# A decode kernel: wo's first 20 heads in one load, part of V's last tile as 112, 8 and 8 partitions, q made as rows, two heads' sums folded together

## The chip, the cores and the metric

The kernel runs on one core of a Trainium2 chip. The metric is the device time of one execution in microseconds (us), as the median of several runs; less is better. The core has five engines with queues of their own: TensorE (PE in the profile, with PEld for its weight loads), VectorE (DVE), ScalarE (ACT), GpSimd (POOL) and SyncE (SP). SP issues nearly all DMAs of this kernel; the DMA engines, 16 of them, carry them out.

## The reference

One token attends to a cache, beside a small feed-forward block, and a gate mixes the two. All data are bf16.

```python
# x: [1, 1, 512]; k_cache, v_cache: [1, 32, 65536, 128]; wq: [512, 4096]; wo: [4096, 512]
# w_gate, w_up: [512, 1792]; w_down: [1792, 512]; gate_w: [512]
q = (x @ wq).reshape(1, 1, 32, 128)                       # 32 heads
p = softmax(einsum(q, k_cache) * 128 ** -0.5)             # per head, over 65536 keys
a = einsum(p, v_cache).reshape(1, 1, 4096) @ wo
b = (silu(x @ w_gate) * (x @ w_up)) @ w_down
g = sigmoid((x * gate_w).sum(-1, keepdims=True))
out = g * a + (1 - g) * b
```

The two caches are 1,074 MB, and each element is used once. The whole input is 1,088 MB.

## The kernel before

**Tiling.** A head's keys are split over the 128 partitions, 512 to each, and a head is done in G = 2 tiles of SIZE = 256 keys per partition. So there are N = 64 tiles of K and 64 of V, each 128 partitions x 64 KB (8 MB). They go through a ring of SLOTS = 3 buffers of that size. A buffer is free again when the last instruction that reads its tile has ended, and `load` then issues the next tile's DMA from SP. The order of all work is written out by hand; each engine does its instructions in program order.

**The loop** (line 485) runs over n = 0 to 63. Iteration n loads K's tile n and V's tile n - 2 (LEAD = 2). `products` multiplies the K tile in place with q, which `query_spread` has copied to all partitions, on VectorE, and folds the 128 products of a key to 16 by three additions (lines 258 and 262). `scores` adds those 16 up and moves them to PSUM with eight matmuls (line 271); after them the K tile's buffer is free. `add_up` makes the scores of them. When a head's two tiles are scored (n even), `row_max` and `exponentials` make the softmax weights P_sb. They are placed behind the first multiplication of the next K tile; for that the tile is cut in rows 0 to 64 and 64 to 256. `values` multiplies a V tile with P_sb in 64 matmuls of four columns (line 340), which go to four strips of O_ps in turn; after them the V tile's buffer is free.

**A head's end.** `head_copy` copies O_ps to SBUF; `head_sum` adds its pieces up with four matmuls against `pick` (float32: each is two instructions), for one head at a time. `head_row` scales the head's row of 128 and puts it into a row of QUAD = 4 heads; `turn` turns four heads' row into columns of oT by small matmuls, as the lhsT that `into_row` needs for the projection with wo.

**wo** (4,096 rows of 512, 1 KB each) comes in four parts. Heads 0 to 3 (FIRST, 512 rows) are loaded in mid-run by `load_tall`: after the V loads at ten values of n, four DMAs each, of 5, 3 or 1 partitions four apart, in rows of 3 to 5 KB; `tall_row` and `tall_zero` clear their buffers on GpSimd, `turn_first` turns these heads' values, and `project_tall` projects them. Heads 4 to 19 (LONG) are one load of 128 rows of 16 KB, after the last V tile but one; 20 to 27 (PAIR) and 28 to 31 (LAST) come at the end.

**q.** `query_columns` makes q as 32 columns, one per head, with 128 matmuls of one column; `query_spread` makes a diagonal matrix from a head's column on ScalarE (diag_q) and copies it to all partitions with one matmul.

**The end** (from line 534). The last V tile is loaded in three parts by V_CUTS, 168, 64 and 24 keys per partition (rows of 43,008, 16,384 and 6,144 B), behind LONG's wo, then PAIR and LAST. `values` runs part by part, O_ps is folded on VectorE (line 574), the last head's value goes to oT, the rest of wo is projected, and the row is copied and stored.

Of the kernel before, what the change touches and what calls it, by code (L numbers as in the profile page):

```python
# [11 lines left out]
P = 128  # L12
# [12 lines left out]
FIRST, LONG, PAIR, LAST = (0, 4), (4, 20), (20, 28), (28, 32)  # L25

SHARES = ((5, 3), (3, 15), (1, 4))
TALL_ROUNDS = ((2, 0, 4), (1, 0, 5), (1, 5, 10), (1, 10, 15), (0, 0, 3))
TALL_LOADS = {14: 0, 23: 1, 32: 2, 41: 3, 50: 4}
TALL_PROJECTS = {18: 0, 27: 1, 36: 2, 45: 3, 54: 4}  # L30
# [3 lines left out]
def kernel(  # L34
# [31 lines left out]
    qT = edge.tile([P, H], f32, name="qT")  # L66
# [22 lines left out]
    x_row = consts.tile([1, D], bf16, name="x_row", tag="o_row")  # L89
# [4 lines left out]
    def load(dst, cache, n, name, cuts=None):  # L94
        t, taken[name, n] = big(name)
        view = t.rearrange("p (j d) -> p j d", d=Dh)
        src = cache[0, n // G, :, :].rearrange("(p j) d -> p j d", p=P)
        a = n % G * SIZE
        cuts = cuts or (0, SIZE)
        for c, d in zip(cuts[:-1], cuts[1:]):  # L100
            nc.sync.dma_start(out=view[:, c:d, :], in_=src[:, a + c : a + d, :])
        dst[n] = view
# [30 lines left out]
    def query_columns(first, last):  # L133
        q_ps = psum_m.tile([P, last - first], f32, name="q_ps", tag="misc")
        for h in range(first, last):
            for t in range(KT):
                nc.tensor.matmul(
                    q_ps[:, h - first : h - first + 1],
                    lhsT=wq_sb[:, t, h * Dh : (h + 1) * Dh],
                    rhs=xT[:, t : t + 1],  # L140
                    start=(t == 0),
                    stop=(t == KT - 1),
                )
        nc.scalar.activation(out=qT[:, first:last], in_=q_ps, func=ACT.Copy)
# [3 lines left out]
    def query_spread(h):  # L148
        diag_q = consts.tile([P, Dh], bf16, name="diag_q")
        nc.scalar.activation(out=diag_q, in_=ident_b, func=ACT.Copy, scale=qT[:, h : h + 1])  # L150
        qb_ps = psum_m.tile([P, Dh], f32, name="qb_ps", tag="misc")
        nc.tensor.matmul(qb_ps, lhsT=ones_b, rhs=diag_q, start=True, stop=True)  # L152
        q_tiles[h] = pair.tile([P, Dh], bf16, name="q_sb")
        nc.scalar.activation(out=q_tiles[h], in_=qb_ps, func=ACT.Copy)  # L154
# [3 lines left out]
    query_columns(0, 1)  # L158
    query_spread(0)
    query_columns(1, H)  # L160
# [18 lines left out]
    gw_row = consts.tile([1, D], bf16, name="gw_row", tag="tall")  # L179
# [69 lines left out]
    def products(n, a, b):  # L249

        K = K_tiles[n][:, a:b, :]
        qb = q_tiles[n // G]
        q_rep = bass.AP(
            tensor=qb.tensor,
            offset=qb.offset,
            ap=[list(qb.ap[0]), [0, b - a], [1, Dh]],
        )
        yield nc.vector.tensor_tensor(out=K, in0=K, in1=q_rep, op=ALU.mult)  # L258
# [92 lines left out]
    def head_copy():  # L351
        O_sb = consts.tile([P, QUAD * Dh], f32, name="O_sb")
        nc.scalar.activation(out=O_sb, in_=O_ps, func=ACT.Copy)  # L353
        return [O_sb[:, c * Dh : (c + 1) * Dh] for c in range(QUAD)]

    def head_sum(h, parts):
        if h >= LAST[0]:
            r_ps = psum_r.tile([P, 1], f32, name="r_ps")
            for c in range(QUAD):
                nc.tensor.matmul(  # L360
                    r_ps, lhsT=parts[c], rhs=pick[:, c : c + 1], start=(c == 0), stop=(c == 3)
                )
            return r_ps
        r_ps = psum_r.tile([1, Dh], f32, name="r_ps")
        for c in range(QUAD):
            nc.tensor.matmul(  # L366
                r_ps, lhsT=pick[:, c : c + 1], rhs=parts[c], start=(c == 0), stop=(c == 3)
            )
        return r_ps


    row0 = 0
    TP = 32 + 4 * SHARES[0][0]
    assert sum(2 * 4 * ports * deep for ports, deep in SHARES) == QUAD * P
    TR = max(b - a for _, a, b in TALL_ROUNDS)
    pieces, bases = [], []
    width = 0
    for ports, deep in SHARES:
        bases.append(width)
        for half in range(2):  # L380
            pieces.append((row0, row0 + 4 * ports * deep, width + 32 * half * deep))
            row0 += 4 * ports * deep
        width += TP * deep
    tallT = consts.tile([TP, sum(deep for _, deep in SHARES)], bf16, name="tallT")
    tall = {}

    def tall_row():
        tall["row"] = consts.tile([1, width], bf16, name="tall_row", tag="tall")
        nc.gpsimd.memset(tall["row"], 0.0)

    def tall_zero():
        tall["sb"] = consts.tile([TP, TR, D], bf16, name="tall_sb", tag="tall")
        nc.gpsimd.memset(tall["sb"], 0.0)

    def load_tall(r, half):
        s, a, b = TALL_ROUNDS[r]
        ports, deep = SHARES[s]
        first = pieces[2 * s + half][0]
        for i in range(4):
            src = bass.AP(  # L400
                tensor=A_wo.tensor,
                offset=A_wo.offset + (first + i * deep + a) * D,
                ap=[[4 * deep * D, ports], [1, (b - a) * D]],
            )
            lo = 32 * half + i
            nc.sync.dma_start(
                out=tall["sb"][lo : lo + 4 * (ports - 1) + 1 : 4, : b - a].rearrange(
                    "p t n -> p (t n)"
                ),
                in_=src,  # L410
            )

    def project_tall(r):
        s, a, b = TALL_ROUNDS[r]
        rows = 32 + 4 * SHARES[s][0]
        at = sum(deep for _, deep in SHARES[:s])
        for t in range(b - a):
            into_row(tallT[:rows, at + a + t : at + a + t + 1], tall["sb"][:rows, t, :])
# [3 lines left out]
    def head_row(h, r_ps):  # L422
# [4 lines left out]
        if h < FIRST[1]:  # L427
            for a, b, at in pieces:
                lo, hi = max(a, h * Dh), min(b, h * Dh + Dh)
                if lo < hi:  # L430
                    nc.scalar.activation(
                        out=tall["row"][:, at + lo - a : at + hi - a],
                        in_=r_ps[:, lo - h * Dh : hi - h * Dh],
                        func=ACT.Copy,
                        scale=gate[0:1, :],
                    )
            return
        if h % QUAD == 0:
            rows[h // QUAD] = consts.tile([1, QUAD * Dh], bf16, name="o_row")
        at = (h % QUAD) * Dh  # L440
        nc.scalar.activation(
            out=rows[h // QUAD][:, at : at + Dh], in_=r_ps, func=ACT.Copy, scale=gate[0:1, :]
        )

    def turn_first():
        t_ps = psum_m.tile([TP, tallT.shape[1]], f32, name="t_ps", tag="misc")
        c = 0
        for s, (ports, deep) in enumerate(SHARES):
            src = tall["row"][:, bases[s] : bases[s] + TP * deep]
            for t in range(deep):  # L450
                nc.tensor.matmul(
                    t_ps[:, c + t : c + t + 1],
                    lhsT=src.rearrange("o (p t) -> o t p", t=deep)[:, t, :],
                    rhs=one_b,
                    start=True,
                    stop=True,
                )
            c += deep
        nc.scalar.activation(out=tallT, in_=t_ps, func=ACT.Copy)

    def turn(g):
        if g == 0:
            turn_first()
            return
        first, last = LONG if g * QUAD < LONG[1] else PAIR
        deep = last - first
        tall_of = QUAD * P // deep
        lo = (g * QUAD - first) // QUAD * tall_of
        t_ps = psum_m.tile([P, deep], f32, name="t_ps", tag="misc")
        o_row = rows.pop(g).rearrange("o (p t) -> o t p", t=deep)  # L470
# [14 lines left out]
    for n in range(N):  # L485
# [3 lines left out]
        if v is not None:  # L489
            load(V_tiles, A_v_cache, v, "V_t")  # L490
            for half in range(2):
                if n - half in TALL_LOADS:
                    load_tall(TALL_LOADS[n - half], half)
# [3 lines left out]
        cuts = K_CUTS.get(n) or ((0, SIZE) if top_of is None else (0, 64, SIZE))  # L497
        vector = (i for a, b in zip(cuts[:-1], cuts[1:]) for i in products(n, a, b))
        r_ps = None
        if done is not None:  # L500
            r_ps = head_sum(done, head_copy())
# [8 lines left out]
        if n == 1:  # L510
            feed_forward_out(*ff)
            free.append(gu_slot)
            tall_row()
        if n % G:
            add_up(n - 1)
        if r_ps is not None:
# [3 lines left out]
        if group is not None:  # L520
            turn(group)
            if group == 0:
                tall_zero()
# [3 lines left out]
        if n in TALL_PROJECTS:  # L527
            project_tall(TALL_PROJECTS[n])
        group = None
        if done is not None and done % QUAD == QUAD - 1 and done < LAST[0]:  # L530
            group = done // QUAD
# [14 lines left out]
    load(V_tiles, A_v_cache, N - 1, "V_t", V_CUTS[N - 1])  # L546
# [10 lines left out]
    r_ps = head_sum(H - 2, head_copy())  # L557
# [62 lines left out]
```

## Time and profile before

| | us |
|---|---|
| median of 3 runs | 2521.13 (2520.9 to 2521.15) |
| the profiled execution | 2520.96 |
| its span in the profile | 2519.1 |
| VectorE busy in it | 2185.8 (87%) |
| TensorE busy in it (weight loads beside it) | 698.7 (28%) |
| ScalarE, GpSimd busy in it | 95.1 (4%), 4.0 |

HBM reads are 1087.64 MB, 432 GB/s over the span. The span is what the profiler saw from the first to the last instruction; the device time has some 2 us more around it.

How to read the lines below. A line of the chain of waits names what the end waited for, followed back from the last instruction, with its share of the span. A line of the queues has packets, MB and the share of the 16 engines' span. A line of the timeline has its start in us from the span's start, the us that it took (several merged instructions have a count, x8), the engine, the line of the program, the operation, what it wrote and read, and in brackets how long the engine was idle before it and what ended that. The trace also has a record of every DMA packet, with start, duration, size and queue, but not its engine.

### The profile page before, as it was taken

To read this page: it belongs to the slowest core of one execution; us is meant where nothing else is said; L and a number is where in the kernel's file an instruction comes from. 1 tells how busy PE (TensorE), PEld (TensorE's weight loads), DVE (VectorE), ACT (ScalarE), POOL (GpSimd) and SP (SyncE) were. 2 spreads that over 40 slices of the span, in tenths; PEclk is the share of its full clock that TensorE was granted. 3 is DMA by queue.
4 is the path that set the end of the run, shared out by engine and by line. 5 is a ranking of instruction groups with operands and counts; after the bars stand their busy time and mean duration, and the time that the engine had idled before them with its cause. 6 is when DMAs were issued, how large, how long until landed. Compare 5 with 4: busy or idle time off the path is not lost.

```text
span 2519.1 us, 12218 instructions
## 1 busy us (share of the span) xinstructions
PE 698.7 (28%) x5422; PEld 252.0 (10%) x5422; DVE 2185.8 (87%) x599; ACT 95.1 (4%) x277; POOL 4.0 (0%) x8
## 2 busy tenths in 40 slices
PE   2132222223222222232222322322323223223224
PEld 2010000101001000010000100110100001001011
DVE  6998998888988889888899888898888988889984
ACT  0000000000000000000000000000000000000000
POOL 0000000000000000000000000000000000000000
PEclk9566556656566566665665665656555666656566
DMA  9999999999999999999999999999999999999998
GB/s 419 435 433 433 437 437 433 432 433 435 432 433 434 434 433 433 435 434 433 434 437 432 432 433 433 434 433 434 434 434 433 434 434 433 434 436 432 432 432 378
DMA packets 20875, 1088.41 MB, mean 432 GB/s; under 512 B 2396, under 2 KB 2912, under 8 KB 3416
## 3 DMA queue, kind: packets, MB, share of 16 engines
q1 hardware_dynamic: 20822, 1087.65, 99.7%
q8 instruction: 42, 0.69, 0.1%
q14 instruction: 9, 0.07, 0.0%
q10 hardware_dynamic: 2, 0.00, 0.0%
HBM read 1087.64 MB, written 0.00 MB: 432 GB/s over the span
## 4 chain that ended last, share of the span: by engine, by line
DMA 84%; PE 14%; DVE 1%; issue 0%; SPq 0%; ACT 0%; DVEq 0%
DMA V_t<-in_A_v_cache_dram 81%; PE O_ps L340 14%; DMA wo_t<-in_A_wo_dram 2%; DMA K_t<-in_A_k_cache_dram 1%; DVE K_t L258 1%; DVE K_t L262 1%; PE part_ps L271 0%; PE b_ps L227 0%; SPq L88 0%; ACT out_sb L588 0%; PE a_ps L186 0%; PE g_ps L231 0%; DVEq L258 0%
## 5 line engine op out<-in xcount | busy, mean ns | idle before, releaser
L258 DVE TENSOR_TENSOR K_t<-K_t,q_sb 128x8192 bf16<-128x8192 bf16 (+4 forms) x97 | 1107.3, 11416 | 245.2 <-DMA K_t<-in_A_k_cache_dram 245.2
L262 DVE TENSOR_TENSOR K_t<-K_t 128x4096 bf16<-128x4096 bf16 (+8 forms) x291 | 1001.5, 3441 | 9.0
L340 PE MATMUL O_ps<-V_t,P_sb 128*4 128x512 bf16 x4096 | 365.5, 534 | 923.9 <-DMA V_t<-in_A_v_cache_dram 923.8
L271 PE MATMUL part_ps<-K_t,ident_b 128*128 128x512 bf16 x512 | 230.6, 605 | 611.1 <-DVE K_t L262 611.1
L340 PEld LDWEIGHTS <-P_sb 128*4 128x4 bf16 x4096 | 122.7, 110 | 1160.7 <-issue 1075.5
L271 PEld LDWEIGHTS <-ident_b 128*128 128x128 bf16 x512 | 59.9, 117 | 753.0 <-issue 752.9
L306 PE MATMUL mT_ps<-diag,ones_f 128*128 128x129 f32 (+1 forms) x64 | 25.3, 497 | 215.9 <-ACT diag L303 215.9
L287 DVE TENSOR_REDUCE S_sb<-part_ps 128x256 f32<-128x512 f32 x64 | 43.7, 683 | 3.5 <-PE part_ps L271 3.5
L313 DVE TENSOR_REDUCE top<-mT_ps 128x1 f32<-128x128 f32 x32 | 9.3, 291 | 42.1 <-PE mT_ps L306 42.1
L154 ACT ACTIVATE q_sb<-qb_ps 128x128 bf16<-128x128 f32 x32 | 8.9, 277 | 940.2 <-PE qb_ps L152 940.2
L353 ACT ACTIVATE O_sb<-O_ps 128x512 f32<-128x512 f32 x31 | 18.4, 595 | 581.4 <-PE O_ps L340 581.4
L366 PE MATMUL r_ps<-O_sb,pick 128*1 128x128 f32 x224 | 40.3, 341 | 0.0
L306 PEld LDWEIGHTS mT_ps<-diag,ones_f 128*128 128x128 f32 x64 | 15.8, 307 | 227.1 <-ACT diag L303 227.1
L303 ACT ACTIVATE diag<-ident_b,m 128x128 f32<-128x128 bf16 x32 | 12.8, 401 | 577.3 <-DVE m L301 577.3
L366 PEld LDWEIGHTS r_ps<-O_sb,pick 128*1 128x1 f32 x224 | 20.3, 100 | 32.5 <-issue 22.5
L317 ACT ACTIVATE P_sb<-S_sb,bias 128x512 bf16<-128x512 f32 x32 | 23.1, 722 | 1.2
L301 DVE TENSOR_REDUCE m<-S_sb 128x1 f32<-128x512 f32 x32 | 22.0, 686 | 1.1
L574 DVE TENSOR_SCALAR fold<-O_ps,pick 128x128 f32<-128x128 f32 x1 | 0.4, 351 | 23.4 <-PE O_ps L340 23.4
L201 PE MATMUL gu_ps<-xT,gu_t 128*128 128x1 bf16 x112 | 7.0, 198 | 21.2 <-DMA gu_t<-in_B_w_gate_dram 20.5
L150 ACT ACTIVATE diag_q<-ident_b,qT 128x128 bf16<-128x128 bf16 x32 | 12.3, 385 | 0.0
L201 PEld LDWEIGHTS <-gu_t 128*128 128x128 bf16 x112 | 6.9, 158 | 21.4 <-DMA gu_t<-in_B_w_gate_dram 20.6
L186 PE MATMUL a_ps<-b_sb,ones_f 1*1 1x256 f32 x4 | 1.0, 606 | 28.6 <-ACT b_sb L245 28.6
(68 smaller groups left out, 112.6 us busy)
## 6 DMA issues: line engine op xcount, KB each, us to landing
K_t<-in_A_k_cache_dram SPq DMA_DIRECT2D x2, 4096.0 KB
V_t<-in_A_v_cache_dram SPq DMA_DIRECT2D x1, 5376.0 KB
K_t<-in_A_k_cache_dram SPq DMA_DIRECT2D x1, 5120.0 KB
wq_t<-in_A_wq_dram SPq DMA_DIRECT2D x1, 4096.0 KB
K_t<-in_A_k_cache_dram SPq DMA_DIRECT2D x1, 3072.0 KB
wo_t<-in_A_wo_dram SPq DMA_DIRECT2D x1, 2048.0 KB
V_t<-in_A_v_cache_dram SPq DMA_DIRECT2D x1, 2048.0 KB
gu_t<-in_B_w_gate_dram SPq DMA_DIRECT2D x1, 1792.0 KB
```

The source lines that it names most:

```text
L201: nc.tensor.matmul(gu_ps[:, w * FT + ft : w * FT + ft + 1], lhsT=cols[:, t, ft, :], rhs=xT[:, t : t + 1], start=(t == 0), stop=(t == KT - 1),)
L258: yield nc.vector.tensor_tensor(out=K, in0=K, in1=q_rep, op=ALU.mult)
L262: yield nc.vector.tensor_tensor(out=K[:, :, 0:half], in0=K[:, :, 0:half], in1=K[:, :, half : 2 * half], op=ALU.add,)
L271: nc.tensor.matmul(part, lhsT=ident_b, rhs=K_tiles[n][:, :, c : c + wide], start=(c == 0), stop=(c == WIDTH - wide),)
L287: nc.vector.tensor_reduce(out=S_tiles[h][:, a : a + SIZE], in_=S_parts.pop(n), axis=AXIS.X, op=ALU.add)
L301: nc.vector.tensor_reduce(out=m, in_=S_tiles[h], axis=AXIS.X, op=ALU.max)
L303: nc.scalar.activation(out=diag[:, :P], in_=ident_b, func=ACT.Copy, scale=m)
L306: nc.tensor.matmul(mT_ps[:, :wide], lhsT=ones_f, rhs=diag[:, :wide], start=True, stop=True)
L317: nc.scalar.activation(out=P_tiles[h], in_=S_tiles[h], func=ACT.Exp, bias=bias, scale=scale, accum_out=new_sum(h),)
L340: nc.tensor.matmul(O_ps[strip : strip + QUAD, :], lhsT=P_tiles[h][:, a + j : a + j + QUAD], rhs=V_tiles[n][:, j : j + QUAD, :], start=(a + ...
L353: nc.scalar.activation(out=O_sb, in_=O_ps, func=ACT.Copy)
L366: nc.tensor.matmul(r_ps, lhsT=pick[:, c : c + 1], rhs=parts[c], start=(c == 0), stop=(c == 3))
```

## The change

Five edits, in one step:

- The special path for heads 0 to 3 goes, with its loads, buffers and projections. LONG is now heads 0 to 19, one load of 128 rows of 20 KB. Heads are turned in groups of five (and of four in PAIR).
- The first part of V's last tile is loaded as three DMAs, partitions 0 to 111, 112 to 119 and 120 to 127, one after the other.
- q is made as four rows, on partitions 0, 32, 64 and 96, 512 columns at a time: 32 matmuls with x as the weights. `query_spread` copies a head's piece of a row to all partitions with a matmul against a row of ones; the diagonal matrix goes.
- `head_copy` keeps two heads side by side, and `head_sum` adds both up, 256 columns wide, at the second.
- `products` multiplies a tile with a softmax in it in two halves of 128 rows, and then adds over the whole tile in three instructions instead of twice three.

```diff
-FIRST, LONG, PAIR, LAST = (0, 4), (4, 20), (20, 28), (28, 32)
-SHARES = ((5, 3), (3, 15), (1, 4))
...
+LONG, PAIR, LAST = (0, 20), (20, 28), (28, 32)
+GROUPS = ((0, 5), (5, 10), (10, 15), (15, 20), (20, 24), (24, 28))
+UNEVEN = {(63, 0): (0, 112, 120, 128)}
...
-    qT = edge.tile([P, H], f32, name="qT")
+    q_rows = edge.tile([97, H * Dh // 4 + Dh // 2], bf16, name="q_rows")
...
-        for c, d in zip(cuts[:-1], cuts[1:]):
-            nc.sync.dma_start(out=view[:, c:d, :], in_=src[:, a + c : a + d, :])
+        for i, (c, d) in enumerate(zip(cuts[:-1], cuts[1:])):
+            parts = uneven.get((n, i), (0, P))
+            for p, q in zip(parts[:-1], parts[1:]):
+                nc.sync.dma_start(out=view[p:q, c:d, :], in_=src[p:q, a + c : a + d, :])
...
+    def query_row(i, c):
+        if c not in q_ps:
+            q_ps[c] = psum_m.tile([97, BANK], f32, name="q_ps", tag="misc")
+        at = i * q_wide + c * BANK
+        row = q_ps[c][32 * i : 32 * i + 1, :]
+        for t in range(KT):
+            nc.tensor.matmul(
+                row,
+                lhsT=xT[:, t : t + 1],
+                rhs=wq_sb[:, t, at : at + BANK],
+                start=(t == 0),
+                stop=(t == KT - 1),
+            )
+        nc.scalar.activation(
+            out=q_rows[32 * i : 32 * i + 1, c * BANK : (c + 1) * BANK], in_=row, func=ACT.Copy
+        )
...
-        diag_q = consts.tile([P, Dh], bf16, name="diag_q")
-        nc.scalar.activation(out=diag_q, in_=ident_b, func=ACT.Copy, scale=qT[:, h : h + 1])
         qb_ps = psum_m.tile([P, Dh], f32, name="qb_ps", tag="misc")
-        nc.tensor.matmul(qb_ps, lhsT=ones_b, rhs=diag_q, start=True, stop=True)
+        nc.tensor.matmul(
+            qb_ps,
+            lhsT=ones_b[32 * i : 32 * i + 1, :],
+            rhs=q_rows[32 * i : 32 * i + 1, at : at + Dh],
+            start=True,
+            stop=True,
+        )
...
-    query_columns(0, 1)
+    query_row(0, 0)
     query_spread(0)
-    query_columns(1, H)
+    for c in range(q_wide // BANK):
+        for i in range(4):
+            if i or c:
+                query_row(i, c)
...
-        yield nc.vector.tensor_tensor(out=K, in0=K, in1=q_rep, op=ALU.mult)
+        for c in range(parts):
+            k = K[:, c * some : (c + 1) * some, :]
+            yield nc.vector.tensor_tensor(out=k, in0=k, in1=q_rep, op=ALU.mult)
...
+    def head_copy(h):
+        if h % 2 == 0 or h >= LAST[0]:
+            O_sbs[0] = consts.tile([P, 2, QUAD * Dh], f32, name="O_sb")
+        both = O_sbs[0]
+        nc.scalar.activation(out=both[:, h % 2, :], in_=O_ps, func=ACT.Copy)
+        return both
...
-        r_ps = psum_r.tile([1, Dh], f32, name="r_ps")
+        if h % 2 == 0:
+            return None
+        r_ps = psum_r.tile([1, 2 * Dh], f32, name="r_ps")
         for c in range(QUAD):
             nc.tensor.matmul(
-                r_ps, lhsT=pick[:, c : c + 1], rhs=parts[c], start=(c == 0), stop=(c == 3)
+                r_ps,
+                lhsT=pick[:, c : c + 1],
+                rhs=both[:, :, c * Dh : (c + 1) * Dh],
+                start=(c == 0),
+                stop=(c == QUAD - 1),
             )
...
-            for half in range(2):
-                if n - half in TALL_LOADS:
-                    load_tall(TALL_LOADS[n - half], half)
...
-        cuts = K_CUTS.get(n) or ((0, SIZE) if top_of is None else (0, 64, SIZE))
-        vector = (i for a, b in zip(cuts[:-1], cuts[1:]) for i in products(n, a, b))
+        cuts = K_CUTS.get(n, (0, SIZE))
+        parts = 1 if top_of is None else 2
+        vector = (i for a, b in zip(cuts[:-1], cuts[1:]) for i in products(n, a, b, parts))
...
-        if n in TALL_PROJECTS:
-            project_tall(TALL_PROJECTS[n])
...
-    load(V_tiles, A_v_cache, N - 1, "V_t", V_CUTS[N - 1])
+    load(V_tiles, A_v_cache, N - 1, "V_t", V_CUTS[N - 1], UNEVEN)
```

## The prediction

> **What bounds the kernel now.** I read the page first: the chain that ended last, then the DMA and GB/s slices, then the queues.
>
> ```profile
> DMA 84%; PE 14%; DVE 1%; issue 0%; SPq 0%; ACT 0%; DVEq 0%
> DMA  9999999999999999999999999999999999999998
> q1 hardware_dynamic: 20822, 1087.65, 99.7%
> q8 instruction: 42, 0.69, 0.1%
> q14 instruction: 9, 0.07, 0.0%
> ```
>
> The DMA engines are full from end to end (q1: 99.7% of 16 engines' span). In the trace's packet records nearly all of the 16,000 packets of 65,536 B take 2.418 us, 27.1 GB/s, and the next packet of an engine starts 4 ns before the last ends. So packets can be strung into 16 engines, each with its own list of work, and the last of them sets the end. VectorE (87%) matters only if it lets them run dry. For that I read a stretch of the timeline in mid-run:
>
> ```profile
> 1015.42 4.42 DVE L258 TENSOR_TENSOR K_t<-K_t,q_sb 128x8192 bf16<-128x8192 bf16 x1 [6.82 <-DMA K_t<-in_A_k_cache_dram]
> 1023.06 0.72 ACT L317 ACTIVATE P_sb<-S_sb,bias 128x512 bf16<-128x512 f32 x1
> 1034.68 5.65 PE L340 MATMUL O_ps<-V_t,P_sb 128*4 128x512 bf16 x64 [12.22 <-DMA V_t<-in_A_v_cache_dram]
> 1040.38 0.33 SPq L101 DMA_DIRECT2D V_t<-in_A_v_cache_dram  x1
> 1053.95 17.22 DVE L258 TENSOR_TENSOR K_t<-K_t,q_sb 128x32768 bf16<-128x32768 bf16 x1 [2.06 <-DMA K_t<-in_A_k_cache_dram]
> ```
>
> VectorE waits for K (6.82, 2.06 us), TensorE for V (12.22). V's next load is issued at 1040.38, 13.6 us before the load ahead of it lands (1053.95): no engine runs dry. At the end that changes:
>
> ```profile
> 2480.55 3.60 PE L271 MATMUL part_ps<-K_t,ident_b 128*128 128x512 bf16 x8 [7.22 <-DVE K_t L262]
> 2484.18 1.28 SPq L101 DMA_DIRECT2D V_t<-in_A_v_cache_dram  x3
> 2492.67 23.13 DMA wo_t<-in_A_wo_dram
> 2515.85 0.29 PE a_ps L186 x2
> 2516.16 0.38 ACT out_sb L588
> ```
>
> V's last tile takes the slot of K's last, which those eight matmuls release at 2484.15. Its first packets start at 2485.24, and three engines have by then been idle for 1.4 to 2.9 us, the only idle time after the start. The last wo data land just before 2515.85; what follows takes 3.3 us to the span's end, 2519.1.
>
> **The engines' lists.** The 42 code fetches of 16,384 B (q8) fall on eight engines in a fixed round. Each takes 0.93 us and makes the packet behind it 0.49 longer, less a little overlap: 1.39. The k-th comes when TensorE has issued about 256 k instructions (the 20th at 5,050, the 42nd at 10,688 of 10,872). So eight engines ("loaded") lose 5 x 1.39 = 7 us, and two of them, with a sixth fetch at 2473.9 and 2498.6, 8.3. The rows of load_tall lie on five of the other eight ("light"). Positions, from the packets: first row of V's last tile at 2490.5 to 2490.9 on loaded engines (2492.26 with six fetches). From there every engine has 8 rows of 43,008 B at 1.586 (12.69) and 10.60 of smaller packets. That gives 2490.89 + 12.69 + 10.60 = 2514.18 for the slowest with five fetches, and 2515.54 and 2515.38, the two last ends of all, for those with six.
>
> **The change, part by part.**
> *wo as one load.* Each of the 128 rows grows from 16 to 20 KB: 8 x 4,096 B per engine at 27.1 GB/s, +1.21 us for all 16. The 40 small loads and their 120 rows go (up to 6.7 us on a light engine), with their 44 projections, 22 turns and two memsets. Light engines come earlier, but not the loaded ones, which set the end.
> *112, 8 and 8.* 112 rows split sevenfold; if both pieces of 8 go to the light engines, these have 9 rows and the loaded ones 7: -1.59 us on loaded, +1.59 on light. The trace has no 8-row load. Bounds: -1.59 (as said), +1.59 (both pieces on the loaded eight). I take -1.59, since the nearest rows, the loads of 5, 3 and 1 rows, all fell on light engines. SP issues two more DMAs, 0.33 to 0.43 us each, during 30 us of queued data: nothing.
> *Fewer instructions.* TensorE matmuls: q 128 to 32, folded sums 224 to 112, tall and turns 202 to 160 (22 + 80 + 44 + 56 against 96 + 64): 250 fewer, two instructions each. 10,372 / 256 gives 40 fetches, five for each loaded engine. That takes 1.39 off the two that end last.
> *q as rows.* A 1x512 matmul took 3.33/14 = 0.24 us (L227), a 1x512 copy on ScalarE 0.68 (L245). The first row is spread by about 15.5, and K's first part lands at 21.9. All eight are done between 20.6 (no row waits for a copy) and 28 (all do). SP's loads of the feed-forward weights, behind the wq slot, move from 17.54 to there, and with them K's second tile in SP's queue. K's first tile keeps the engines busy until 31, so nothing; past about 30, every us would count in full. Later the removed diag_q copy (0.385 on ScalarE) only shortens a wait.
> *products in two halves.* Multiplying 128 rows (8.68) ahead of the softmax instead of 64 (4.43) moves P_sb 4.25 later, to 1028.0; V lands at 1034.68, so 6.6 is left; beyond that V's slot and next load would be late. VectorE saves 33.3 - 32.8 = 0.5 us a head, which becomes wait for K.
> *Folded sums.* Eight matmuls of twice the width for two heads, at most 2 us instead of 1.03, and two copies of 0.34, within TensorE's 12 us wait for V: nothing. Projecting 40 instead of 32 columns before V's last tile costs 0.5 us inside a 9.17 wait.
>
> **Sum.** The slowest loaded engine: 2490.89 + 1.21 + 7 x 1.586 + 10.60 = 2513.80. Light ones start at 2485.24, lose 0.9 to the first packet as now, and end at 2485.24 + 0.9 + 14.27 + 10.6 = 2511.0. One light engine carries five of the nine 8 KB fetches (q14, 0.84 each); it ends its share of V's last tile but one at 2483.89, 0.9 of that for 24 rows of load_tall: 2483.0 + 6.08 (wo, 8 x 20 KB) + 14.27 + 10.6 = 2513.95 at most. Against 2515.54 the end moves by -1.74 (-1.6 by that last engine). V's smaller parts land earlier by as much, so fold and projection follow. The profiled execution, 2520.96 (span 2519.1), becomes 2519.2; the median lies 0.17 higher: **2519.4**. Its own range: 2518.6 (0.8 more from a better packing) to 2521.0 (fetches not fewer).
>
> **Rivals.**
> *Rows that meet in one group of partitions (slower).* In a 128-row load each engine has partitions of its own: load_tall lays engine k's rows at 4k to 4k+3 and 32 higher, and I take such eight as a group. The pieces of 8 give eight neighbouring partitions to eight engines, four to a group. If a group takes only what one engine brings, 1.586 becomes 6.34 per row. Light engines after seven rows, 2497.2, then 12.7, then 10.6: 2520.5, +5.0. The 112 rows in sevens also put ten engines into the eight groups of partitions 0 to 63. Stepping all rows with equal shares gives 2525.8, against 2515.4 for the present kernel stepped alike: +10.5, **2531.6**. It decides (over 0.2%) if a group carries less than about 1.3 engines' rate; at twice the rate it is +2, at four times nothing. For it: the output's two rows, from partitions 0 and 32, ran on two engines at once, so engines follow the row's index and not its partition. Against it: no row shows two engines at one group, and 27.1 GB/s can be the engine's own limit.
> The Trainium skill, SBUF — State Buffer, section "Door 1: The DMA port swizzle", speaks for it: bandwidth goes by the ports that the partitions reach, eight partitions to a port, and 4 partitions measured 27.6 GB/s. By that rule the time would be this rival's; the trace neither confirms nor denies it.
> *Split without effect.* Engines keep 8 rows each: 2514.18 + 1.21 = 2515.39, -0.15: 2521.0. The two-engine output speaks against it.
> *The pieces fall on the loaded engines:* 2514.18 + 1.21 + 1.59 = 2516.98, +1.4: 2522.6. The small loads speak against it.
> The Trainium skill, DMA: Bandwidth & Descriptors, section "Why a DMA increments its semaphore by 16 and not by 1", puts such a load on the lowest-numbered engines, as many as divide its rows; the loads of 5, 3 and 1 rows agree.
>
> **How the numbers follow.** Forecast 0.45; meeting rows 0.44 (0.40 beyond 0.2%, 0.04 milder); no effect 0.05; loaded side 0.03; a cover that fails 0.03. A difference under 0.2% (5 us) counts as none. Slower: 0.40 + 0.03 = 0.43. Faster 0.02, off the forecast's share: the 16 ends average 2512.8, so perfect balance is worth 2.7 us, and only a mistake of mine gets there. Same: 0.43 + 0.04 + 0.05 + 0.03 = 0.55. The range has to hold forecast and first rival: 2518.4 to 2532; above it lies a worse meeting (rows dealt in turn).
>
> **What would show it.** Right: 40 fetches on q8; packets of 43,008 B all at 1.59 us; the two partitions' pieces on engines without fetches; last wo landing at 2514. Wrong: packets of 43,008 B that take 3 to 6.4 us, a landing of V's last tile after 2505.4, engines idle in mid-run, or K's second tile late.

## The result, and the profile after

| | before | after |
|---|---|---|
| median, us | 2521.14 (2520.9 to 2521.15, 4 runs) | 2549.73 (2549.0 to 2550.72, 4 runs) |
| span of the profiled execution, us | 2519.1 | 2548.9 |
| last row of 43,008 B lands, us | 2504.95 | 2534.13 |
| last data of wo land, us | 2515.80 | 2545.50 |

The ratio is 1.0114, 95% interval 1.0096 to 1.0131: 28.6 us slower. The forecast was 2519.4, the first rival 2531.6, the range up to 2532. The changed kernel's page has, in the order chain, DMA slices, queues:

```profile
DMA 52%; DVE 42%; PE 5%; issue 0%; ACT 0%; SPq 0%
DMA  9999999999999999999999999999999999999998
q8 instruction: 40, 0.66, 0.1%
```

The DMA slices still show full engines, so they do not show the loss: an engine that moves data half as fast is as busy. The 40 code fetches are as forecast. The timeline of the end shows where the time went:

```profile
2481.73 3.60 PE L289 MATMUL part_ps<-K_t,ident_b 128*128 128x512 bf16 x8 [7.87 <-DVE K_t L280]
2485.36 2.00 SPq L101 DMA_DIRECT2D V_t<-in_A_v_cache_dram  x5
2487.40 43.94 SPq L496 DMA_DIRECT2D wo_t<-in_A_wo_dram  x5
2535.33 5.97 PE L358 MATMUL O_ps<-V_t,P_sb 128*4 128x512 bf16 x58 [29.89 <-DMA wo_t<-in_A_wo_dram]
2541.79 0.60 PE L358 MATMUL O_ps<-V_t,P_sb 128*4 128x512 bf16 x6 [0.49 <-DMA V_t<-in_A_v_cache_dram]
2545.86 0.38 ACT L541 ACTIVATE out_sb<-a_ps 33x256 bf16<-33x256 f32 x1 [0.97 <-PE a_ps L201]
```

The eight matmuls that release the buffer end only 1.2 us later than before (2485.34 against 2484.15), and V's five loads follow at once. But TensorE gets V's first part after 29.89 us of waiting instead of 9.17, as the kernel before has it:

```profile
2505.38 5.91 PE L340 MATMUL O_ps<-V_t,P_sb 128*4 128x512 bf16 x58 [9.17 <-DMA V_t<-in_A_v_cache_dram]
```

(In the changed kernel the releaser is printed as wo; in the packet records the last row of 43,008 B lands at 2534.13.) The chain of waits, in order of time, says the same: the loads of V, then what queues behind them.

```profile
2448.94 17.24 DVE K_t L276
...
2485.36 0.33 SPq L101
...
2485.74 45.26 DMA V_t<-in_A_v_cache_dram
...
2531.02 14.48 DMA wo_t<-in_A_wo_dram
```

What the engines moved in between is in the view by windows; its last three columns are TensorE's granted clock, the busy share of the DMA engines and GB/s:

```profile
2487.00:2497.00 10.00, 6.06 (x68) 2.49 (x69) 0.85 (x5) 1.38 (x5) 0.00 (x0) 0.83 1.08 233
2497.00:2507.00 10.00, 4.43 (x40) 2.42 (x39) 0.00 (x0) 0.00 (x0) 0.00 (x0) 0.63 0.97 211
2508.00:2520.00 12.00, 0.00 (x0) 0.00 (x0) 0.00 (x0) 0.00 (x0) 0.00 (x0) 0.50 0.99 129
2520.00:2534.00 14.00, 0.00 (x0) 0.00 (x0) 0.00 (x0) 0.00 (x0) 0.00 (x0) 0.50 0.90 238
```

The same two first windows of the kernel before:

```profile
2487.00:2497.00 10.00, 7.86 (x98) 3.73 (x99) 0.78 (x5) 1.17 (x4) 0.00 (x0) 0.70 1.03 443
2497.00:2507.00 10.00, 1.62 (x16) 0.52 (x19) 0.00 (x0) 0.00 (x0) 0.00 (x0) 0.64 0.96 411
```

So all sixteen engines run at half speed while the 112 rows come (most rows of 43,008 B take 3.1 to 3.5 us instead of 1.59) and at under a third with the pieces of 8 (up to 6.05 us). And from 2487.5 the rows of wo, 20,480 B, which other engines still write to their own partitions, take 1.5 us instead of 0.76.

A second, small loss is at the start. The four matmuls of a q row take 1.87 us, and every row but one waits for ScalarE's copy of the row before, as the four rows of a bank share a PSUM tile; only the last row of the first bank and the first of the second run side by side:

```profile
26.53 1.87 PE L142 MATMUL q_ps<-wq_t,xT 128*1 128x512 bf16 x4 [0.67 <-ACT q_rows L149]
28.43 0.59 ACT L149 ACTIVATE q_rows<-q_ps 1x512 bf16<-1x512 f32 x1 [1.95 <-PE q_ps L142]
29.07 1.87 PE L142 MATMUL q_ps<-wq_t,xT 128*1 128x512 bf16 x4 [0.67 <-ACT q_rows L149]
30.97 0.33 SPq L190 DMA_DIRECT2D gu_t<-in_B_w_gate_dram  x1
32.77 0.85 SPq L101 DMA_DIRECT2D K_t<-in_A_k_cache_dram  x2
```

The weights' load leaves at 30.97 instead of 17.54, the DMA engines are idle for 0.1 to 1.5 us near 32, and VectorE gets K's last tile at 2448.94 instead of 2447.76.

### The profile page after: what moved, and what is told of

Its sections match the earlier page's. It is cut to its first block, busy times and chain, and to the rows that moved or that the text cites. A ratio compares the mean times of both kernels' runs of the same rounds, so it can differ in the third digit from the quotient of the medians.

```text
span 2548.9 us, 11539 instructions
## 1 busy us (share of the span) xinstructions
PE 706.3 (28%) x5172; PEld 238.7 (9%) x5172; DVE 2174.0 (85%) x506; ACT 89.2 (3%) x245; POOL 0.7 (0%) x6
## 4 chain that ended last, share of the span: by engine, by line
DMA 52%; DVE 42%; PE 5%; issue 0%; ACT 0%; SPq 0%
DMA K_t<-in_A_k_cache_dram 49%; DVE K_t L276 22%; DVE K_t L280 20%; PE part_ps L289 4%; DMA V_t<-in_A_v_cache_dram 2%; DMA wo_t<-in_A_wo_dram 1%; PE q_ps L142 1%; DMA wq_t<-in_A_wq_dram 0%; ACT q_rows L149 0%; DVE S_sb L305 0%; PE mT_ps L324 0%; DVE m L319 0%; SPq L195 0%; SPq L193 0%; SPq L191 0%
## 5 line engine op out<-in xcount | busy, mean ns | idle before, releaser
L276 DVE TENSOR_TENSOR K_t<-K_t,q_sb 128x16384 bf16<-128x16384 bf16 (+2 forms) x97 | 1107.4, 11417 | 260.5 <-DMA K_t<-in_A_k_cache_dram 260.5
L280 DVE TENSOR_TENSOR K_t<-K_t 128x16384 bf16<-128x16384 bf16 (+5 forms) x198 | 987.1, 4985 | 6.8
L394 PE MATMUL r_ps<-O_sb,pick 128*1 128x256 f32 x112 | 34.2, 461 | 0.0
L142 PE MATMUL q_ps<-wq_t,xT 128*1 128x512 bf16 x32 | 13.1, 620 | 14.7 <-DMA wq_t<-in_A_wq_dram 10.7
L394 PEld LDWEIGHTS r_ps<-O_sb,pick 128*1 128x1 f32 x112 | 9.6, 95 | 29.3 <-issue 23.6
L158 PE MATMUL qb_ps<-q_rows,ones_b 1*128 1x128 bf16 x32 | 8.4, 262 | 0.7 <-ACT q_rows L149 0.7
```

What stands on the lines that cost most here:

```text
L142: nc.tensor.matmul(row, lhsT=xT[:, t : t + 1], rhs=wq_sb[:, t, at : at + BANK], start=(t == 0), stop=(t == KT - 1),)
L276: yield nc.vector.tensor_tensor(out=k, in0=k, in1=q_rep, op=ALU.mult)
L280: yield nc.vector.tensor_tensor(out=K[:, :, 0:half], in0=K[:, :, 0:half], in1=K[:, :, half : 2 * half], op=ALU.add,)
L394: nc.tensor.matmul(r_ps, lhsT=pick[:, c : c + 1], rhs=both[:, :, c * Dh : (c + 1) * Dh], start=(c == 0), stop=(c == QUAD - 1),)
```

## The experiments

All times are medians of several runs with a range, or one run where none is given. "Meet" means: write to the same group of eight partitions (4k to 4k+3 and 32 higher) at the same time. "Early" engines are those that run no code fetch and come to V's last tile first.

**Which part costs.** e1: the changed kernel, with the first part of V's last tile whole again. e2: the kernel before with the split alone.

```diff
-UNEVEN = {(63, 0): (0, 112, 120, 128)}
+UNEVEN = {}
```

> The changed kernel with the first part of V's last tile as one load of 128 partitions. Theory A (the split alone made the loss, the other edits give their small sums): packets of 43,008 B back at 1.59 us; against the kernel before, -1.4 us (two code fetches fewer on the engines that end last), +1.2 (wo's 4 KB more per row on every engine), +1.2 (K's tiles land 1.2 us later throughout, since the q rows hold the feed-forward weights' loads back past the end of K's first tile): 2522 us, 2521 to 2523. Rival B (another edit shares in the loss, in mid-run): above 2526.

Measured: 2521.75 (2521.19 to 2523.43), ratio to the kernel before 1.0004 [0.9995, 1.0014]. Rows of 43,008 B take 1.59 us again.

e2's edit:

```diff
+PARTS = [(slice(p, q), slice(p, q)) for p, q in ((0, 112), (112, 120), (120, 128))]
+WHOLE = ((slice(0, P), slice(0, P)),)
...
-            nc.sync.dma_start(out=view[:, c:d, :], in_=src[:, a + c : a + d, :])
+            for rows, from_rows in (PARTS if name == "V_t" and n == N - 1 and c == 0 else WHOLE):
+                nc.sync.dma_start(out=view[rows, c:d, :], in_=src[from_rows, a + c : a + d, :])
```

> The kernel before with nothing changed but the first part of V's last tile, as loads of 112, 8 and 8 partitions. Theory A: the loss stays with the split, packets of 43,008 B at 3.1 to 3.3 us in the 112 and 4 to 6 us in the pieces of 8, and the time is 2545 to 2552 us. Rival B (the split costs only beside the other edits, because the light engines come earlier there): packets near 1.6 to 2.5 us, below 2535.

Measured: 2542.86 (2542.41 to 2544.76), ratio 1.0086 [1.0069, 1.0103]; last row of 43,008 B at 2528.28. Its rows of that size take 1.8 to 5.8 us, and the time is some 2 us under theory A's range. Its timeline has TensorE's wait for V's first part, which was 9.17 us in the kernel before:

```profile
2529.53 5.50 PE L344 MATMUL O_ps<-V_t,P_sb 128*4 128x512 bf16 x58 [26.60 <-DMA V_t<-in_A_v_cache_dram]
```

So the split is the loss: 21.9 us on the kernel before, 28.0 on the changed one. That it costs more there fits that all early engines come to it together, while in the kernel before the rows of load_tall let only four come first; this was not tried by itself.

**Where it meets: at the partitions written, or at the rows read.** The kernel before, first part as 16 loads of 8 rows: neighbouring (e3), four apart (e4), then partitions of the tile and rows of the cache by different rules (e5, e6).

```diff
+NEAR = [slice(p, p + 8) for p in range(0, P, 8)]
+APART = [slice(p + c, p + c + 29, 4) for p in range(0, P, 32) for c in range(4)]
+PARTS = list(zip(NEAR, NEAR))     # e3; e4: APART, APART; e5: NEAR, APART; e6: APART, NEAR
```

> The kernel before; the first part of V's last tile as 16 loads of 8 neighbouring partitions, so that all 128 rows of 43,008 B go to eight engines, 16 rows each. Theory 1 (engines that write into one group of eight partitions share one engine's rate): four engines to a group, packets of 5.5 to 6.4 us; that part lands near 2485 + 16 x 6 = 2580, and the time is about 2596 us. Theory 2 (what meets is the source: neighbouring rows, 131,072 B apart, read at once): slow too, without a set factor of four. Theory 3 (any load that isn't 128 rows has slow packets, 3.2 us): 2485 + 51 = 2536, about 2553 us. No meeting at all: 1.6 us, about 2528 us.

> As the run before, but each of the 16 loads takes 8 partitions that are four apart, in the tile and in the cache alike, so that each of the eight engines has a group of its own. Theory 1: packets of 1.59 us, the part lands near 2485.2 + 0.9 + 25.4 = 2511.5 instead of 2505, and the time is 2526 to 2529 us. Theory 2: faster than the neighbouring ones, with no reason for exactly 1.59. Theory 3: 3.2 us, about 2553 us. If an engine also needs its own partitions (those it has in a load of 128) for the full rate, the half of the loads in partitions 64 to 127 shows slower packets than the other half.

> The kernel before, with the first part of V's last tile as 16 loads of 8 rows: the eight rows go to neighbouring partitions of the tile and are read from cache rows four apart (V's keys are so permuted in this part: the output differs there). Theory A, engines share the way into a group of partitions (destination): packets of 43,008 B take 2 to 4.6 us as in the loads of eight neighbouring rows, last one ends near 2540, time 2554 to 2558. Theory B, engines share the source rows (neighbouring stretches of memory): packets at 1.59 until V's second part begins, last end near 2525, time 2540 to 2543.

> The mirror of the run before: the eight rows of a load go to partitions four apart and are read from neighbouring cache rows (V's keys are permuted in this part: the output differs there). Theory A (destination): packets of 43,008 B at 1.59 us until V's second part begins near 2506, 3.2 after that; last end near 2525, time 2540 to 2543. Theory B (source): packets of 2 to 4.6 us from the first, time 2554 to 2558.

| | partitions of a load | cache rows of a load | time, us | rows of 43,008 B |
|---|---|---|---|---|
| e3 | neighbouring | neighbouring | 2556.36 | 3 to 4.6 us, then down to 1.9, 3.3 to 3.8 from 2519 |
| e5 | neighbouring | four apart | 2564.05 | 2.1 to 4.4 us, never 1.59 |
| e4 | four apart | four apart | 2541.45 | 1.59 us until 2506, then 3.2 |
| e6 | four apart | neighbouring | 2541.55 | 1.59 us until 2506, then 3.2 |

What decides is the partitions and not the memory: e4 and e6, with the same partitions and different cache rows, agree to 0.1 us. (e3 and e5 differ only in their cache rows too, and are 7.7 us apart, with one run each; e5 is 6 us over the range expected of it. Why was not followed up.) The change of e4 and e6 at 2506 is the start of V's second part: its 16,384 B rows on the late engines then take 1.28 instead of 0.61 us, since the early engines have come to partitions 64 to 127, where the late ones write. That change was in neither theory for e4, which comes some 12 us after the one that had full speed. e3 was far from the 2596 that strict sharing gave. My reading, which no run shows, is that engines that meet fall out of step, and those ahead move on to another group.

**The q rows.** e7 is e1 with each row in a tile of its own:

```diff
-        if c not in q_ps:
-            q_ps[c] = psum_m.tile([97, BANK], f32, name="q_ps", tag="misc")
...
+        q_ps = psum_m.tile([97, BANK], f32, name="q_ps", tag="misc")
```

> The changed kernel with V's first part whole, and every q row in a PSUM tile of its own, so that no row's matmuls wait for ScalarE's copy of the row before. Theory A (the q rows hold up the feed-forward weights, behind them K's second tile, and the engines run dry for about 1.2 us near 32 us): the weights' load is issued by 29 us instead of 31, no engine idles at 32, K's last tile lands near 2447.8, time 2520.3 to 2520.8 against 2521.75 of the same kernel with shared tiles. Rival (the idle time is made good later, or the matmuls of 0.47 us alone keep the load late): the weights' load not before 30.5, time 2521.5 to 2522.

Measured: 2521.01 (2520.73 to 2521.72), ratio 1.0 [0.9991, 1.0009]; its timeline:

```profile
18.30 3.66 PE L140 MATMUL q_ps<-wq_t,xT 128*1 128x512 bf16 x16 [0.24 <-ACT q_rows L147]
21.99 0.33 SPq L188 DMA_DIRECT2D gu_t<-in_B_w_gate_dram  x1
2447.83 17.23 DVE L274 TENSOR_TENSOR K_t<-K_t,q_sb 128x32768 bf16<-128x32768 bf16 x1 [2.62 <-DMA K_t<-in_A_k_cache_dram]
```

Sixteen matmuls now take 3.66 us, the load leaves 9 us earlier, no engine idles after 30, and the 1.2 us at K's last tile are back. The medians of e1 and e7 differ by 0.74 us; the two intervals overlap, so it is the traces that show this loss. Its size is not fixed: in e1's own trace, with the same q rows as the changed kernel, four matmuls at 23.62 took only 1.02 us, the load left at 29.75, no engine ran dry near 32, and K's last tile came at 2448.43, so the wait cost 0.6 us there.

**Moving work to the early engines without a meeting.** e8 is e7 with wo's first four heads as loads of 8 partitions four apart.

```diff
...
+    first_sb = wo_t[0:32, LAST[1] * D : (LAST[1] + DEEP) * D]
+    first_src = A_wo[: FIRST[1] * P, :].rearrange("(p t) n -> p (t n)", t=DEEP)
+    for c in range(4):
+        nc.sync.dma_start(out=first_sb[c : c + 29 : 4, :], in_=first_src[c : c + 29 : 4, :])
```

> The kernel of the run before, but wo's first four heads come apart from the rest as four loads of 8 partitions four apart (16 rows of wo, 64 KB, a partition; 32 partitions), behind the load of heads 4 to 20: 8 x 4,096 B fewer on every engine, four rows of 64 KB more on the eight engines without code fetches. Theory: these rows go at full rate as no engine shares a group of partitions with another, the two last engines lose 1.2 us, the light ones gain 8.4 us and stay in front: end near 2514.3 instead of 2515.5, time 2519.0 to 2519.8, a little faster than the kernel before. Rival (rows of 8 partitions meet the rest at a group, as with V's second part in the loads four apart): packets of 65,536 B at over 2.42, light engines last, time 2522 to 2526.

Measured: 2521.88 (2521.81 to 2522.29), ratio 1.0003 [0.9994, 1.0012]. The expectation had sizes wrong: a row is 16,384 B and an engine gets four, 2.4 us in all, not 9.7. These ran at full speed (0.61 us a row), and seven late engines began V's tile 1.2 us earlier, at 2490.4 to 2490.9 or before. But the eighth late engine began at 2492.97, 2.4 us late, and one early engine ended wo early and stood idle for 1.6: the eight engines that such a load takes are not the eight early ones, one is late. That one now ends last. Neither theory had this.

**Does a meeting hurt those who meet nobody?** In the changed kernel's trace, rows of wo were slowed that met none of V's. e9, e10, e15, e13 and e14 take e7 and put two loads of 32,768 B rows, which nothing reads, behind wo's first. In e9, e10 and e15 a load has two rows, in e13 and e14 four; within each set only their partitions differ. (More rows alone do not slow the engines: e8's four loads of eight rows ran at full speed.)

```diff
+    for i, rows in enumerate((slice(64, 77, 4), slice(65, 78, 4))):     # e13
+        nc.sync.dma_start(
+            out=wo_t[rows, H * D : H * D + 32 * D],
+            in_=A_wo[128 * i : 128 * i + 128, :].rearrange("(p t) n -> p (t n)", t=32),
+        )
```

> The kernel with V's first part whole and q rows in tiles of their own, and two loads more behind wo's first: each brings two rows of 32,768 B, which nothing reads, to unused bytes of wo's tile, at partitions 0 and 4, then 1 and 5. These are the partitions that engines 0 and 1 write in a load of 128 rows. Every theory: 2.4 us more for these two engines, which are early, and no other packet changes: packets of 20,480 B stay at 0.76 us, time 2521.0 (at most 2521.6 if one of the two is the engine with the 8 KB fetches).

> The same two loads, four partitions higher: 4 and 8, then 5 and 9, so that engine 1 writes where engine 2 is writing its own rows. Theory A (only engines that write the same group of partitions slow down): two or three early engines lose 2.4 to 5 us, packets of 20,480 B on the others stay at 0.76 us, time 2521.0 to 2521.6. Theory B (one such meeting holds up all sixteen engines): for some 4.8 us from 2484.8 every packet takes twice its time (20,480 B in 1.5 us), all engines lose 2.4 us, time 2523.2 to 2523.8.

> The same with two rows to a load, to partitions 64 and 65, then 96 and 97: engines 0 and 1 write into the group of engine 8, three engines with it. Theory C: rows of 3.6 us, engine 8's packets 2.3 us, all others untouched. Theory D: a slowing of the others, between that of two in a group (none) and that of five.

> The kernel of the two loads behind wo's first, but each brings four rows of 32,768 B, to partitions 64, 68, 72, 76 and then 65, 69, 73, 77: engines 0 to 3 write into the groups of engines 8 to 11 while these write their own rows of wo, four groups with two engines each. Theory C (two to a group halve each other and nobody else): the eight rows take 2.4 us, the packets of 20,480 B on four engines take 1.5 us for some 4.8 us, on the others 0.76. Theory D (meetings at several groups fill something that all engines share): all packets of that time, the rows of V on engines 4 to 7 and wo's on 12 to 15 too, take twice their time.

> The same, to partitions 64 to 67 and then 96 to 99: engines 0 to 3 all write into the group of engine 8, five engines with it. Theory C: these rows take up to five times 1.2 us (6 us), engine 8's packets of 20,480 B up to 3.8 us, all others stay at 0.76 us and 1.59 us. Theory D: the other engines are slowed too, while it lasts, most of all if the crowd at one group counts and not the number of groups.

Mean GB/s of an engine between 2487 and 2490, worked out from the packet records (27 is full speed; about nine engines are on wo, four to seven on V):

```
                                       added rows   rows of V   rows of wo   all 16     time, us
e9   own groups                              27.0        26.1         26.9      426     2520.9
e10  one group with two engines              15.3        22.9         26.5      387     2520.94
e15  one group with three                    12.1        19.5         24.0      340     2521.27
e13  four groups with two each               13.8        15.6         13.9      231     2525.71
e14  one group with five                      7.3         8.2          7.3      120     2527.96
```

One pair leaves the others alone (e10: four of the 128 rows of wo are slow). The engine with the added rows takes 2.34 and 2.41 us for each instead of 1.21, and the row of V that the group's own engine brings takes 3.24 instead of 1.59. (The other engine's added rows took 1.72 and 1.73, which is not explained.) The third engine at a group in e15 costs the others a tenth in the mean. But with four pairs, or five engines at one group, every engine falls to the rate of those that meet: in e13 at most four of nine engines on wo can meet one, and all nine run at half; in e14 at most one of nine can, and all run at a fourth. The windows from 2487 to 2497 of e10, e13 and e14:

```profile
2487.00:2497.00 10.00, 7.72 (x106) 3.95 (x107) 0.81 (x5) 1.17 (x4) 0.00 (x0) 0.76 1.03 435
```

```profile
2487.00:2497.00 10.00, 6.26 (x66) 2.42 (x67) 0.72 (x5) 1.17 (x4) 0.00 (x0) 0.69 0.99 342
```

```profile
2487.00:2497.00 10.00, 6.24 (x66) 2.41 (x67) 0.67 (x5) 1.17 (x4) 0.00 (x0) 0.70 0.88 212
```

**Which splits meet.** e7 again, with the first part as 64 + 64 (e11), 112 + 16 (e12) and four loads of 32 partitions four apart (e16):

```diff
-UNEVEN = {}
+UNEVEN = {(63, 0): (0, 64, 128)}                                # e11
+UNEVEN = {(63, 0): (0, 112, 128)}                               # e12
+UNEVEN = {(63, 0): [slice(c, c + 125, 4) for c in range(4)]}    # e16
```

> The same kernel without these loads, V's first part as two loads of 64 rows. If rows are dealt in runs (engine k gets rows 4k to 4k+3), the eight early engines, the lowest, write their own groups in the first load and start at 1.59 us a row, until the late ones come near 2492 and write to the same groups; the order in time keeps most of it apart: V's first part ends between 2508 and 2514, time 2524 to 2530. If rows are dealt in turn (row r to engine r mod 16), four engines meet at a group from the first: packets of 6.3 us, last end past 2540, time past 2555.

> The same kernel, V's first part as 112 rows and then 16 rows in one load (one row for each engine, four to a group). Theory B with rows in runs: all packets, wo's last ones too, take twice their time from the first rows of the 112 on (3.2 us for 43,008 B), and near four times at the 16 rows: V's first part ends between 2526 and 2532, time 2541 to 2548. Theory A with rows in runs: most packets of the 112 at 1.59 us, V's first part ends near 2515, time 2530 to 2533.

> The kernel with q rows in tiles of their own, V's first part as four loads of 32 rows four apart, two rows for each engine. If rows are dealt in turn (row r to engine r mod 16), engine k of the lowest eight writes first its own group (4k) and then that of engine k + 8: first packets of 1.59 us, 3.2 later. If they are dealt in runs (2k and 2k + 1 to engine k), engines k and k + 4 meet from the first: packets of 3.2 us at once. Time 2533 to 2541 in both.

Measured: e11 2539.91, all 128 rows at 2.0 to 3.45 us, 3.3 in the median, from the first on, and the rows of wo beside them at 1.4 to 1.6; e12 2544.66, mostly 3.1 to 3.4 us in the 112 and up to 5.8 at the 16 neighbouring rows, the last at 2527.77, as the theory of a common slowing had it; e16 2521.07, rows at 1.59 us, last at 2504.72. The expectations for e11 and e16 both fell: neither dealing that I had thought of gives half speed at once in the one and full speed throughout in the other. e16's line of TensorE's wait for V's first part, and its windows:

```profile
2505.19 4.55 PE L356 MATMUL O_ps<-V_t,P_sb 128*4 128x512 bf16 x42 [8.92 <-DMA V_t<-in_A_v_cache_dram]
```

```profile
2487.00:2497.00 10.00, 8.00 (x106) 3.93 (x106) 0.69 (x5) 1.17 (x4) 0.00 (x0) 0.74 1.03 445
2497.00:2507.00 10.00, 1.81 (x20) 0.70 (x24) 0.00 (x0) 0.00 (x0) 0.00 (x0) 0.60 0.92 395
```

and e11's windows, at half of that:

```profile
2487.00:2497.00 10.00, 6.62 (x66) 2.45 (x67) 0.49 (x3) 1.10 (x4) 0.00 (x0) 0.67 1.06 223
2497.00:2507.00 10.00, 4.43 (x40) 2.43 (x39) 0.00 (x0) 0.00 (x0) 0.00 (x0) 0.50 0.97 204
```

One dealing gives both: the first half of the rows to engines 0 to 7, the second to 8 to 15, in turn by blocks of a 32nd of the rows (four rows of 128, two of 64, one of 32). Then 32 rows four apart fall each on the engine that owns its partitions, as 128 rows do, and of 64 neighbouring rows two engines share each group. That is fitted to e11 and e16, not shown; for 112, of which a 32nd is no whole number, the dealing stays open. No version here is faster than the kernel before by more than can be told.

## Why the prediction was wrong

*The step that failed* is the price of "112, 8 and 8": taken as -1.59 us, it is +28.0 (e1 against the result). "I take -1.59, since the nearest rows, the loads of 5, 3 and 1 rows, all fell on light engines": those rows lie four partitions apart, and the question was not only on which engine a row falls but whose partitions it fills. The same loads of 8 cost nothing four apart while the owners were elsewhere (e4 until 2506).

*The first rival* had the mechanism, and its size was wrong: +10.5 against 28. Its stepping let only engines that meet share a group's rate. The term that fails is the rate of the others, and with it the bound: while several groups are met at once (e13) or one by five engines (e14), all sixteen engines go at the rate of those that meet, so the rest of wo, the 112 rows and V's second part all take twice their time, and three to four times it beside the pieces of 8. Against some 430 GB/s, the windows give a loss of 20 x (1 - 222/430) = 9.7 us from 2487 to 2507, 12 x (1 - 129/430) = 8.4 from 2508 to 2520, and, at 238 GB/s, 14 x (1 - 238/430) = 6.3 from 2520 to 2534: 24 of the 28. The text also held that no row of the trace showed two engines at one group, which was so, and that 27.1 GB/s could be the engine's own limit. It is the group's as well: added rows that met in e10 took 2.34 to 2.41 us for 1.21.

The Trainium skill, "SBUF — State Buffer", section "Door 1: The DMA port swizzle", prices a meeting by the port, and e4 and e10 agree (half speed for two). By that alone the time would have been 2531.6. The Trainium skill, "DMA: Bandwidth & Descriptors", section "Back-pressure in remote DMA", says of transfers between cores that a saturated port holds up engines which share the way to it. e13 and e14 show the like in a core's own loads, with engines at 13.9 and 7.3 GB/s that meet nobody.

*The second rival*, the split without effect, would have been 2521.0; e7, which is the change without the split and without the q wait, is 2521.01. So the rest of the sum holds:

- *40 fetches*: right, five on each late engine.
- *wo as one load, +1.21*: right. The late engines begin V's tile at 2491.6 to 2492.2 in e7, the one that had four fetches by then at 2490.3, against 2490.5 to 2490.9.
- *q as rows, nothing*: wrong by 1.2 us. The bounds for all eight rows, 20.6 and 28, were passed: 30.94, as a row's four matmuls take 1.87 us there, 0.47 each (0.24 was taken from L227's row), and every row but one waits for a copy, 2.5 us for a row. The condition was rightly put ("past about 30, every us would count in full"). Without the waits (e7) they end near 22.
- *Products in halves, folded sums*: right; e7 has K's last tile at 2447.83, within 0.1 us of the kernel before.
- *Two more DMAs on SP, nothing*: hidden here behind the slow rows. SP issues wo's last three loads only at 2500.98, 2527.32 and 2531.02, each when an earlier one lands; the engines were busy all the same until 2530.

Of what the text said would show it wrong, three came: rows of 3 to 6.4 us, a landing after 2505.4, K's second tile late.

## What to carry to other kernels

A load that does not cover all 128 partitions is to be judged by whose partitions it writes: let each engine keep its own (32 rows four apart as in e16, or all 128), or let the owners be idle. When several engines meet, the price can be not theirs alone but that of every transfer in flight (four groups with two each in e13, one with five in e14), so a bound worked out engine by engine can be too low. A busy DMA row in the profile says nothing of this; GB/s by windows, or the time of packets of one size, does.

## What was not expected of the hardware

- Engines that share no group with anyone fell to 13.9 (e13) and 7.3 GB/s (e14), while one pair (e10) or three at one group (e15) left them at 26.5 and 24.0. Where between these the common slowing sets in was not tried.
- Split into 64 + 64 the load takes twice its time, into four times 32 rows four apart none more (e11, e16).
- The four matmuls of a q row start 0.21 to 0.22 us apart where the profile records a granted clock of 1.0, and 0.43 before its first record and after it falls to 0.5. In e1 the row at 23.62, within the record of 1.0, took 1.02 us, the one at 25.32, at 0.5, 1.86. The changed kernel's profile has no record before 59.08, and its rows took 1.87. e7's sixteen in 3.66 us lie partly in its record from 21.07 on, and two rows run side by side there.
